# A local attention and squared-ReLU kernel: in the second block, the swap of the turned probabilities is issued at step 8 of each group in place of step 6 (last group: 5)

## The chip, the cores and the metric

The kernel runs on one core of a Trainium2 chip. Its engines work side by side, each through its own instructions in their order: TensorE (PE, with its weight loads PEld), VectorE (DVE), ScalarE (ACT), GpSimd (POOL) and SyncE (SP), which here does nothing but issue DMAs. The metric is the device time of one execution in microseconds (us). The three runs shown took 788.15, 789.97 and 790.61 us; the median is 789.97 us.

## The reference

Queries, keys and values come as 8 batches x 8 heads x 576 tokens x 64. Tokens are cut into chunks of 64, and each chunk attends to itself alone; the result goes through a two-layer MLP with a squared ReLU.

```python
scores = scale * np.matmul(q_c, k_c.transpose(0, 1, 2, 4, 3))
scores = scores - np.max(scores, axis=-1, keepdims=True)
attn = np.exp(scores)
attn = attn / (np.sum(attn, axis=-1, keepdims=True) + 1e-09)
out = np.matmul(attn, v_c)
...
x = np.ascontiguousarray(attn_out.transpose(0, 2, 1, 3)).reshape(B * S, H * D)
...
h = x @ w_in
r = np.maximum(h, 0.0)
g = s * (r * r) + b
return (g @ w_out).astype(np.float32)
```

There are 4608 tokens (36 blocks of 128), 512 features, and a hidden layer of 2048.

## The kernel before, in words

Everything is float32. A factor of a large product is split into a high and a low part, and three products (high by high, high by low, low by high) take the place of one.

The work is staged by tokens. A first stage handles 512 tokens and meanwhile prepares the weights. Then come four blocks of 1024 tokens. A block runs through steps: 12 matmuls of 128x512 each, first those of the up layer, then 28 of the down layer. Blocks two to four (class `Block`) use a scheme with seven products of half matrices in place of eight. The second stage, the first of the four blocks, is class `Second`, which is what the title calls the second block: its up layer takes 32 steps with the plain weights, and beside it DVE and ACT form the sums of weights that the later products need (`combine`, `combined_hi`, `combined_lo`) and send them to DRAM (`keep_combined`, line 200). All weights stand in DRAM as "kept" tiles; `stream` (line 428) requests them back, 512 KB at a time, into a pool of six buffers named `st`. A request has to wait until TensorE has done with the buffer's last tile.

While a block's steps run, the attention of the following block is computed in four groups of 256 tokens. For a group that starts at step n the table of `plan_attention` (line 580) puts: the loads of q, k and v at n - LEAD, the scores on TensorE at n, the row maximum and its subtraction (DVE) at n + 1, the exponential (ACT) at n + 2, the sum (DVE) at n + 3, the division and the turn (DVE, 32x32 transposes, `pB`, line 282) at n + 4, the swap at n + 6, and the products with the values (`values`, line 298, on TensorE) at n + VALUES, together with their copy out of PSUM by ACT. In `Second` the groups start at steps 4, 18, 30 and 41, and the values follow at n + 10.

The swap finishes the transpose that the turn began: eight DMAs of 64 KB within SBUF move 32-row pieces of `pB` into `pT` (line 291). They are issued by SP like every other large DMA: the requests of weights, the sending of the sums, the loads of q, k and v, the output.

What is written in one step is issued in the order of the list `pre[step]`, and `stream` comes behind it. An engine holds its instructions strictly in this order. SP's DMAs take eight semaphores in turn, and a DMA is issued only when the DMA eight places before it, which had the same semaphore, has landed.

Of the kernel before, what the change touches and what calls it, by code (L numbers as in the profile page):

```python
# [48 lines left out]
def local_attention_then_squared_relu_mlp(ctx: ExitStack, tc, qkv, w, s, b, out):  # L49
# [63 lines left out]
    class Pair:  # L113


        def __init__(self, k):
            self.layer, self.k = sequence[k]
            self.words = self.f = None
# [270 lines left out]

    class Block:  # L390
        UP, TILES, ORDER, GROUPS, LEAD, VALUES, END = 28, 56, (0, 2, 1, 3), (3, 14, 25, 36), 5, None, 9

        def __init__(self, n):
            self.tb0 = 4 + (n - 1) * BLOCK
# [41 lines left out]
        def place(self, layer, i):  # L436
            return PLACE[i]
# [142 lines left out]
        def plan_attention(self, n, a, after):  # L580

            self.at(max(n - self.LEAD, 0), a.load_qk, a.load_v)
            last = after is None
            end = ((self.END, a.values), (self.END + 1, a.x_out)) if last else ((self.VALUES or after - n, a.values, a.x_out),)
            for k, *fs in ((0, a.scores), (1, a.peak, a.sub), (2, a.exp), (3, a.sum), (4, a.norm, a.turn), (5 if last else 6, a.swap), *end):
                self.pre[n + k][:0] = fs

        def plan_following(self, following):
# [29 lines left out]
    class Second(Block):  # L618


        UP, TILES, ORDER, GROUPS, LEAD, VALUES, END = 32, 44, (0, 1, 2, 3), (4, 18, 30, 41), 7, 10, 10
        PLACES = 0, 1, 3, 2

        def operands(self, group, d):
# [8 lines left out]
        def place(self, layer, i):  # L633
            return super().place(layer, i) if layer else self.PLACES[i % 4]

# [275 lines left out]
```

## Time and profile before

| what | number |
|---|---|
| median of three runs | 789.97 us (788.15 to 790.61) |
| the profiled execution's own time | 787.95 us |
| its span, first to last instruction | 786.2 us |
| TensorE busy | 772.8 us, 98% of the span |
| DVE, ACT, POOL busy | 598.4, 444.8, 171.9 us |
| mean granted TensorE clock | 1.000 |

The profile is that of one execution, of 787.95 us. Busy time is what an engine spent in instructions; a wait is idle time ahead of an instruction, with the instruction or DMA that ended it. For a DMA the page gives the time from its issue to its landing. The second block runs from about 129 us to 305 us.

### The profile page before, as it was taken

How to read it: one execution, taken by the hardware profiler on the slowest of the kernel's cores; microseconds unless marked ns; L12 is line 12 of the kernel's file. 1: busy time of each engine (PE TensorE's matmuls, PEld its weight loads, DVE VectorE, ACT ScalarE, POOL GpSimd, SP SyncE). 2: the span in 40 equal slices, each digit the busy share in tenths (PEclk: the TensorE clock that was granted, in tenths of full speed). 3: DMA queues.
4: the chain of work that ended last, by engine and by line, in shares of the span. 5: the costliest groups of instructions: out<-in, count | busy, mean ns of one | idle time of the engine just before them, and what ended most of it. 6: DMA issues, size and time to landing. Idle time of an engine off the chain costs nothing.

```text
span 786.2 us, 13839 instructions
## 1 busy us (share of the span) xinstructions
PE 772.8 (98%) x5562; PEld 637.5 (81%) x5562; DVE 598.4 (76%) x610; ACT 444.8 (57%) x527; POOL 171.9 (22%) x74
## 2 busy tenths in 40 slices
PE   7899999999999999999999999999999999999998
PEld 7778788888887878888888888888888888888886
DVE  6898786978869894868799847786999646679752
ACT  4888774566663744555646444465654545565621
POOL 2444430000000240000374500002574101028000
PEclk9999999999999999999999999999999999999999
DMA  9999989889997588676665787857567665555653
GB/s 336 356 315 308 344 311 332 301 277 350 312 382 256 200 304 306 204 275 220 259 232 208 241 298 255 295 167 289 180 260 257 239 234 196 189 192 194 224 176 124
DMA packets 86978, 204.32 MB, mean 260 GB/s; under 512 B 7940, under 2 KB 38916, under 8 KB 86916
## 3 DMA queue, kind: packets, MB, share of 16 engines
q1 hardware_dynamic: 86768, 203.32, 74.1%
q8 instruction: 44, 0.72, 0.3%
q14 instruction: 18, 0.15, 0.1%
q10 hardware_dynamic: 148, 0.13, 0.0%
HBM read 156.24 MB, written 40.89 MB: 251 GB/s over the span
## 4 chain that ended last, share of the span: by engine, by line
PE 64%; DVE 1%; issue 1%; SPq 1%; DMA 0%; ACT 0%; DVEq 0%; ACTq 0%
PE ps_o L486 22%; PE ps_o L456 19%; PE ps L456 11%; PE ps L486 9%; PE ps_o L502 1%; PE ps_a L238 1%; PE ps_o L298 1%; SPq L291 1%; DMA st<-kept 0%; ACT gh L343 0%; PE ps L298 0%; DVE gl L344 0%; DVE pB L282 0%; DVE p L264 0%; DVE tmp L358 0%
## 5 line engine op out<-in xcount | busy, mean ns | idle before, releaser
L486 PE MATMUL ps_o<-gh,st 128*128 128x512 f32 x608 | 189.8, 390 | 0.3 <-DMA st<-kept 0.3
L344 DVE TENSOR_TENSOR gl<-q,gh 128x1024 fp32r<-128x1024 f32 x112 | 168.2, 1524 | 28.4 <-ACT gh L343 28.1
L473 POOL TENSOR_TENSOR q<-q 128x1024 f32<-128x1024 f32 x24 | 73.9, 3099 | 294.7 <-PE ps_a L238 179.1
L456 PE MATMUL ps_o<-xh,st 128*128 128x512 f32 x432 | 137.7, 389 | 0.0
L486 PEld LDWEIGHTS ps_o<-gh,st 128*128 128x128 f32 x608 | 114.1, 188 | 24.6 <-DMA st<-kept 0.4
L343 ACT CAST gh<-q 128x1024 fp32r<-128x1024 f32 x112 | 113.2, 1047 | 11.4 <-DVE q L473 10.7
L486 PE MATMUL ps_o<-gl,st 128*128 128x512 f32 x304 | 118.3, 389 | 0.0
L461 ACT ACTIVATE q<-q 128x1024 f32<-128x1024 f32 x48 | 50.9, 1061 | 80.3 <-DVE q L358 80.1
L456 PEld LDWEIGHTS ps_o<-xh,st 128*128 128x128 f32 x432 | 81.1, 188 | 16.9
L456 PE MATMUL ps_o<-xl,st 128*128 128x512 f32 x216 | 84.0, 389 | 0.0
L486 PE MATMUL ps<-gh,st 128*128 128x512 f32 x256 | 80.6, 390 | 0.8 <-DMA st<-kept 0.8
L456 PE MATMUL ps<-xh,st 128*128 128x512 f32 x240 | 79.5, 392 | 0.0
L679 ACT ACTIVATE o<-o,bias,sb 128x512 f32<-128x512 f32 x34 | 25.8, 808 | 91.4 <-DVE o L358 91.4
L413 POOL TENSOR_TENSOR xt<-xf 128x512 f32<-128x512 f32 x12 | 32.8, 2736 | 192.0 <-PE ps_o L486 137.7
L358 DVE TENSOR_TENSOR q<-ps_o,tmp 128x1024 f32<-128x1024 f32 x35 | 42.8, 1222 | 32.2 <-PE ps_o L456 27.9
L486 PEld LDWEIGHTS ps_o<-gl,st 128*128 128x128 f32 x304 | 57.1, 188 | 11.6
L152 POOL TENSOR_TENSOR f<-f,raw 128x1024 int32<-128x1024 int32 (+1 forms) x18 | 44.6, 2482 | 67.8 <-DVE f L146 24.0
L486 PEld LDWEIGHTS ps<-gh,st 128*128 128x128 f32 x256 | 48.0, 188 | 11.0 <-issue 0.9
L456 PEld LDWEIGHTS ps<-xh,st 128*128 128x128 f32 x240 | 45.0, 188 | 9.7
L358 DVE TENSOR_TENSOR tmp<-ps_o,tmp 128x1024 f32<-128x1024 f32 x30 | 36.6, 1219 | 20.9 <-PE ps_o L456 15.8
L473 DVE TENSOR_TENSOR q<-q 128x1024 f32<-128x1024 f32 x40 | 48.6, 1219 | 4.4 <-ACT q L462 3.7
L462 ACT ACTIVATE q<-q 128x1024 f32<-128x1024 f32 x48 | 51.0, 1062 | 1.5
(110 smaller groups left out, 1307.0 us busy)
## 6 DMA issues: line engine op xcount, KB each, us to landing
st<-kept SPq DMA_DIRECT2D x212, 512.0 KB, 5.1
qk<-in_qkv_dram SPq DMA_DIRECT2D x36, 512.0 KB, 6.1
raw<-in_w_dram SPq DMA_DIRECT2D x32, 512.0 KB, 6.9
kept<-wh SPq DMA_DIRECT2D x24, 512.0 KB, 8.3
kept<-wl SPq DMA_DIRECT2D x24, 512.0 KB, 8.7
v<-in_qkv_dram SPq DMA_DIRECT2D x36, 256.0 KB, 6.2
out_dram<-o SPq DMA_DIRECT2D x17, 512.0 KB, 3.1
pT<-pB SPq DMA_DIRECT2D x96, 64.0 KB, 2.2
```

Source lines behind the costliest of these rows:

```text
L152: nc.gpsimd.tensor_tensor(out=i, in0=i, in1=low.bitcast(I32), op=ALU.add)
L238: nc.tensor.matmul(out=self.ps[rows, h % 2, i * NHP + hp, :], lhsT=qk[cols, 0, hp, c, :], rhs=qk[cols, 1, hp, c, :], start=True, stop=True)
L343: nc.scalar.copy(out=hi[:, :, cols], in_=parts)
L344: nc.vector.tensor_tensor(out=lo[:, :, cols], in0=parts, in1=hi[:, :, cols].bitcast(F32), op=ALU.subtract)
L358: nc.vector.tensor_tensor(out=to, in0=self.ps[product], in1=x, op=ALU.add)
L413: engine.tensor_tensor(out=to, in0=x, in1=y, op=ALU.subtract)
L456: nc.tensor.matmul(out=to[:, k], lhsT=a[:, cols], rhs=x[:, c, :], start=c == 0 and n == 0, stop=c == 1 and n == 2)
L461: nc.scalar.activation(out=q, in_=q, func=AF.Relu)
L462: nc.scalar.activation(out=q, in_=q, func=AF.Square)
L473: engine.tensor_tensor(out=self.q[to, pp], in0=self.q[x, pp], in1=self.q[y, pp], op=ALU.subtract)
L486: nc.tensor.matmul(out=self.to[:, d], lhsT=a[:, cols], rhs=x[:, k, :], start=pp == 0 and k == 0 and n == 0, stop=pp == NPP - 1 and k == 1 ...
L679: nc.scalar.activation(out=to[:, d], in_=source[:, d], func=AF.Identity, scale=s_col, bias=bias[:, d0 + d:d0 + d + 1])
```

## The change

A table `SWAP` now gives the step of the swap, first for the groups that another group follows, then for the last one. For class `Block` it repeats the old numbers (6 and 5). For `Second` it is 8 and 8: three groups have their swap two steps later, the fourth three steps later.

```diff
     class Block:
         UP, TILES, ORDER, GROUPS, LEAD, VALUES, END = 28, 56, (0, 2, 1, 3), (3, 14, 25, 36), 5, None, 9
+        SWAP = 6, 5
...
-            for k, *fs in ((0, a.scores), (1, a.peak, a.sub), (2, a.exp), (3, a.sum), (4, a.norm, a.turn), (5 if last else 6, a.swap), *end):
+            for k, *fs in ((0, a.scores), (1, a.peak, a.sub), (2, a.exp), (3, a.sum), (4, a.norm, a.turn), (self.SWAP[last], a.swap), *end):
...
         UP, TILES, ORDER, GROUPS, LEAD, VALUES, END = 32, 44, (0, 1, 2, 3), (4, 18, 30, 41), 7, 10, 10
+        SWAP = 8, 8
```

No instruction is added or removed, and on PE, DVE, ACT and POOL the order stays. On SP the eight DMAs of the swap move in four places. The lines below the second insertion are numbered one or two higher in the changed kernel.

On SP, around the second group's swap (steps 23 to 27), before: `qk` and `v` are the loads of the third group, `st` the requests of the first two tiles of the down layer, `kept_1_81` and `kept_2_82` sums of weights on their way to DRAM.

```order
L215 DMA qk<-in_qkv_dram 128x1024 x2
L223 DMA v<-in_qkv_dram 128x512 x2
L291 DMA pT<-pB 32x512 x8
L432 DMA st<-kept_0_84 128x1024
L432 DMA st<-kept_1_85 128x1024
L200 DMA kept_1_81<-wh 128x4x256
L200 DMA kept_1_81<-wl 128x4x256
L200 DMA kept_2_82<-wh 128x4x256
```

The same place in the changed kernel, from the first request on, with the semaphores that each DMA waits for (DMAHW0 to DMAHW7 are the eight that DMAs take in turn):

```order
L433 DMA st<-kept_0_84 128x1024 [waits DMAHW4_49,PE_49]
L433 DMA st<-kept_1_85 128x1024 [waits DMAHW5_49,PE_49]
L200 DMA kept_1_81<-wh 128x4x256 [waits DMAHW6_49,Activation_49]
L200 DMA kept_1_81<-wl 128x4x256 [waits DMAHW7_49,DVE_49]
L291 DMA pT<-pB 32x512 [waits DMAHW0_49,DVE_49]
L291 DMA pT<-pB 32x512 [waits DMAHW1_49]
L291 DMA pT<-pB 32x512 [waits DMAHW2_49]
L291 DMA pT<-pB 32x512 [waits DMAHW3_49]
L291 DMA pT<-pB 32x512 [waits DMAHW4_49]
L291 DMA pT<-pB 32x512 [waits DMAHW5_49]
L291 DMA pT<-pB 32x512 [waits DMAHW6_49]
L291 DMA pT<-pB 32x512 [waits DMAHW7_49]
```

Two requests and one pair of sums, 512 KB each, now stand between the loads and the swap, and the last four swap DMAs share their semaphores with these four.

On SP, around the fourth group's swap (steps 44 to 50), before: all are requests of down-layer tiles but the swap.

```order
L432 DMA st<-kept_1_85 128x1024
L432 DMA st<-kept_2_86 128x1024
L291 DMA pT<-pB 32x512 x8
L432 DMA st<-kept_3_87 128x1024
L432 DMA st<-kept_0_84 128x1024
L432 DMA st<-kept_1_85 128x1024
L432 DMA st<-kept_2_86 128x1024
```

And now:

```order
L433 DMA st<-kept_1_85 128x1024
L433 DMA st<-kept_2_86 128x1024
L433 DMA st<-kept_3_87 128x1024
L433 DMA st<-kept_0_84 128x1024
L433 DMA st<-kept_1_85 128x1024
L291 DMA pT<-pB 32x512 x8
L433 DMA st<-kept_2_86 128x1024
```

Three requests moved in front of the swap. In the first group's place a pair of sums and the four loads of the second group (2.5 MB) moved in front of it; in the third group's two stores of the output and two requests (2 MB).

## Rows read from the trace of the kernel before

**Rows 1.** The page's head and its busy line: busy time, share of the span and count of instructions.

```profile
span 786.2 us, 13839 instructions
PE 772.8 (98%) x5562; PEld 637.5 (81%) x5562; DVE 598.4 (76%) x610; ACT 444.8 (57%) x527; POOL 171.9 (22%) x74
```

**Rows 2.** Who waited for whom, TensorE alone, 120 to 330 us: waiter, its line, what it waited for: total us, times, longest us.

```profile
PE ps L486 <- DMA st<-kept: 0.8, 1, 0.8
PE ps_o L486 <- DMA st<-kept: 0.3, 1, 0.3
```

**Rows 3.** TensorE in order of time: start, duration, line, out<-in, count, and in brackets the idle time before it. The values' products (L298) of the four groups, and the two matmuls that waited; last, from the chain of waits, 96 matmuls (8 steps) without a gap.

```profile
168.64 1.16 PE L298 MATMUL ps_a<-pT,v 64*64 64x64 f32 x64
...
209.36 1.16 PE L298 MATMUL ps_a<-pT,v 64*64 64x64 f32 x64
...
245.55 1.16 PE L298 MATMUL ps_a<-pT,v 64*64 64x64 f32 x64
...
251.04 0.50 PE L486 MATMUL ps_o<-gh,st 128*128 128x512 f32 x1 [0.29 <-DMA st<-kept]
...
278.51 1.16 PE L298 MATMUL ps_a<-pT,v 64*64 64x64 f32 x64
280.43 0.47 PE L486 MATMUL ps<-gh,st 128*128 128x512 f32 x1 [0.76 <-DMA st<-kept]
...
283.43 21.76 PE ps_o L486 x96
```

**Rows 4.** SP in order of time: start and duration of the issue, line, out<-in, count. The surroundings of the four swaps (L291).

```profile
151.06 1.69 SPq L432 DMA_DIRECT2D st<-kept  x2
155.55 5.51 SPq L291 DMA_DIRECT2D pT<-pB  x8
...
198.20 0.48 SPq L223 DMA_DIRECT2D v<-in_qkv_dram  x1
201.64 4.95 SPq L291 DMA_DIRECT2D pT<-pB  x8
206.69 1.03 SPq L432 DMA_DIRECT2D st<-kept  x2
...
231.29 1.74 SPq L432 DMA_DIRECT2D st<-kept  x2
236.57 6.81 SPq L291 DMA_DIRECT2D pT<-pB  x8
...
244.66 3.13 SPq L432 DMA_DIRECT2D st<-kept  x4
...
271.76 4.95 SPq L291 DMA_DIRECT2D pT<-pB  x8
276.81 2.96 SPq L432 DMA_DIRECT2D st<-kept  x6
```

**Rows 5.** DVE in order of time: the turns of the second and the fourth group.

```profile
200.37 1.25 DVE L282 STREAM_TRANSPOSE pB<-p 128x1024 f32<-128x1024 f32 x1
...
270.49 1.25 DVE L282 STREAM_TRANSPOSE pB<-p 128x1024 f32<-128x1024 f32 x1
```

**Rows 6.** DMA issues by line in narrow stretches: out<-in, count, KB each, us from issue to landing. In this order: the second request issued from 152.42 us; the v load issued at 198.20; the request issued at 231.29; the request issued at 244.66; a pair of sums issued from 161.16. Then the landing times (min/median/max) of the swaps issued from 201.64 and from 271.76.

```profile
st<-kept SPq DMA_DIRECT2D x1, 512.0 KB, 5.5
...
v<-in_qkv_dram SPq DMA_DIRECT2D x1, 256.0 KB, 7.8
...
st<-kept SPq DMA_DIRECT2D x1, 512.0 KB, 9.8
...
st<-kept SPq DMA_DIRECT2D x1, 512.0 KB, 6.3
...
kept<-wh SPq DMA_DIRECT2D x1, 512.0 KB, 3.2
kept<-wl SPq DMA_DIRECT2D x1, 512.0 KB, 4.8
...
DMA to landing us min/median/max: 2.0/3.8/4.7
...
DMA to landing us min/median/max: 2.0/2.0/2.0
```

**Rows 7.** Stretches: us, then busy time of PE, PEld, DVE, ACT, POOL with counts, the granted TensorE clock, the DMA engines' busy share, and GB/s.

```profile
156.00:162.00 6.00, 6.00 (x29) 4.95 (x28) 5.37 (x11) 3.04 (x3) 0.00 (x0) 1.00 0.44 120
162.00:168.00 6.00, 6.00 (x28) 4.99 (x27) 2.62 (x4) 3.97 (x4) 0.00 (x0) 1.00 0.97 287
192.00:198.00 6.00, 6.00 (x28) 4.95 (x28) 4.96 (x8) 3.80 (x5) 0.00 (x0) 1.00 0.88 249
198.00:204.00 6.00, 6.00 (x28) 4.99 (x27) 5.09 (x9) 0.99 (x2) 0.00 (x0) 1.00 1.05 395
```

**Rows 8.** TensorE's clock: the first matmuls of the run and some 10 us later the same shape (start, duration, count); a stretch behind the last matmul (columns as in rows 7); and TensorE's longest wait in the first 120 us (columns as in rows 2).

```profile
1.05 3.57 PE L107 MATMUL ps_h<-ones 128*128 128x128 f32 x16 [1.05 <-DVE one_col L93]
...
10.33 2.94 PE L107 MATMUL ps_h<-ones 128*128 128x128 f32 x24
...
785.00:787.00 2.00, 0.00 (x0) 0.00 (x0) 0.00 (x0) 0.00 (x0) 0.00 (x0) 0.73 0.00 0
...
PE ps_h L703 <- DVE g L716: 2.5, 2, 1.4
```

## The prediction

> **What bounds the kernel now.** I read the page's busy line first: TensorE is busy 772.8 of 786.2 us [rows 1]. What it does is not changed, so the time can only move by TensorE's idle time. The view of waits comes next, for TensorE alone and the second block: from 120 to 330 us it waited for a DMA twice, 0.8 and 0.3 us [rows 2]. In order of time these are 0.76 us ahead of 280.43 and 0.29 us ahead of 251.04, both for requested weights [rows 3]. More than 1.05 us cannot be won in this block. SP's timeline says where the two come from: SP stands at a swap until its turn is done (fourth group: the turn ends at 270.49 + 1.25 = 271.74, the swap starts at 271.76), spends 5 us on its eight issues, and only then hands out six requests, from 276.81 [rows 4, 5]. The request that landed at 251.0 (244.66 + 6.3) also stood behind a swap, the third [rows 4, 6]. The third thing to read is the other side: how long before the values' products a swap was complete. Those products start at 168.64, 209.36, 245.55 and 278.51 [rows 3]; a swap DMA lands 2.0 us or more after its issue [rows 6].
>
> **The change part by part.** No instruction is added, so durations stay; what moves is SP's order. For each group I follow two questions: do the requests that now go first remove a wait, and does the swap still land before its products?
>
> *Requests in front, third and fourth group.* The two waits of 0.29 and 0.76 us were for the first request behind a swap. Both requests now go ahead of it, several us before they are needed: gain 1.05 us, at the least 0. What is late next: the request now first behind the fourth swap goes out at 276.8 as the first one did, for a matmul three steps later; a step takes 21.76 / 8 = 2.72 us [rows 3], so it has 8.2 us more. Nothing.
>
> *Fourth group's swap.* It waited for the turn, not for its place. Three requests now precede it; the last needs TensorE to have finished step 47, which it does three steps before the values open step 51: 278.51 - 3 x 2.72, at about 270. The swap still starts at 271.76 with the turn and ends its landing at 276.12 + 2.0 = 278.1, before 278.51. Cost 0; the cover is thin (0.4 us), but it was thin before.
>
> *Second group's swap, the term that decides.* Before, SP was free at 198.7 and idled until the turn ended at 201.62 [rows 4, 5]. The eight issues took until 206.6 and the last landed at about 208.0, 1.3 us before the products at 209.36. Now two requests and a pair of sums go first. Their data are ready, and they leave between 198.7 and about 201.7. But the swap pays in another way: each of its DMAs waits until the DMA eight places before it has landed, as the semaphores in the order show, and for the last four these are now the four new ones, 2 MB. They queue behind the loads, whose last one landed at 198.20 + 7.8 = 206.0 [rows 6]. The stretch 198 to 204, where the DMA engines were full with loads and sums alike, moved 395 GB/s [rows 7], so 512 KB take 1.33 us, and four take 5.3: the last of the sums lands at 211.3. Then the eighth swap DMA goes, and lands 2.0 us later, at 213.3. TensorE, which holds its order, stands at the values from 209.36: 4.0 us. Nothing covers that: all later matmuls are queued behind them, and ACT's copy of the values and what DVE takes from later steps wait in turn. On SP the swap holds up more sums and the requests for tiles that TensorE needs from step 34 on, five steps later; and whoever takes over the buffer of `pB` stands some steps later in its engine's order too.
> The bounds: if the four had no queue before them and landed like a pair of sums in a nearly empty one (3.2 and 4.8 us [rows 6]), they would be down by about 206 and only SP's issues would count: the fourth swap DMA starts at 206.0 with the last load's landing, four more follow at 4.95 / 8 = 0.62 us, the last lands at 210.5, and the wait is 1.2 us. If they crawled as in 192 to 198 (249 GB/s, 2.1 us each [rows 7]), it would be 206.0 + 8.4 + 2.0 - 209.36 = 7.1 us. I take 4.0, by the row nearest in time and mix.
>
> The Trainium skill (DMA: Bandwidth & Descriptors, Anatomy of one DMA) gives a fixed cost of about 2.0 us for a DMA plus its bytes at 436 GB/s. The swaps that had the queue to themselves agree on the fixed part (2.0/2.0/2.0 in the fourth group [rows 6]). On the moving part the row says 395: by the page, as an estimate, four tiles take 4.8 us, the wait would be 3.5 us and the sum below +2.4.
>
> *First group's swap.* SP idled from 152.75 to 155.55 for the turn [rows 4]; now a pair of sums and four loads, 2.5 MB, leave in that gap, and the swap behind them. The last request before them landed at 152.42 + 5.5 = 157.9 [rows 6]. At 395 GB/s 2.5 MB take 6.6 us: 164.6, the last swap DMA lands at 166.6, two us before 168.64. At 287 GB/s (162 to 168 [rows 7]) it is 9.1 us, 169.0, and a wait of 0.4. I take 0, with 0.4 as the end. The DMA engines stood at 0.44 in 156 to 162 [rows 7], so the early requests use time that was lost.
>
> *Third group's swap.* The request at 231.29 landed 9.8 us later, at 241.1 [rows 4, 6], and one more request, two stores and two requests now stand between it and the swap's end: five times 1.33 gives 247.8, and 249.8 for the last swap DMA, against products at 245.55 + 4.0 = 249.55. But the wait of the second group lets the queue drain against TensorE, and with no backlog the limit is the second request: free when step 36 is done, three steps before the values (245.55 - 3 x 2.72 + 4.0 = 241.4), and down 5.5 to 6.3 us later [rows 6], 246.9 to 247.7, so that the swap ends at 248.9 to 249.7. So 0 to 0.3 beside the delay of the second group, and I take 0.
>
> The sum: + 4.0 - 1.05 = + 2.95 us, from the profiled execution's 787.95 to 790.9. That execution lies 2.0 us under the median of the runs (789.97); on the median the forecast is 792.9 us.
>
> **The rivals.**
> *A. The swap is in time and only the gain is left (not slower).* The mechanism: DMAs on one queue overlap enough that the four new ones land with the loads in front of them, not after. For it: sums in a nearly empty queue landed after 3.2 and 4.8 us [rows 6], and the DMA engines' share fell to 0.44 during a swap before, so there is room. Against it: the loads in front landed after 7.8 us, which is a queue. With the low bound's wait of 1.2 the sum is +0.15, 790.1 us; with none, 788.9. It decides at the landing of the second sum: at 207.3 or sooner the wait is gone.
> *B. More than one group is late.* If the queue runs at the slow rates in all places: 0.4 in the first group, 7.1 in the second, 0.3 in the third, less 1.05: +6.8, 796.7 us. For it: 249 and 287 GB/s stretches stand right beside two of the four places [rows 7]. Against: those stretches hold gaps in the supply, which the change fills.
> *C. The wait costs TensorE its clock.* In the run's first matmuls 16 of 128x128 took 3.57 us, 0.22 each; later 24 took 2.94, 0.12 each [rows 8]: the two levels, 1.2 and 2.4 GHz. TensorE's longest wait in the first 120 us was 1.4 us, and its clock stayed up; behind the last matmul the granted clock fell to a mean of 0.73 within 785 to 787 [rows 8]. A wait of 4.0 us lies between. If it brings the clock down for as long as the first burst lasted, 3.6 us, half of that is lost: 1.8 us on top, +4.75, 794.7 us. The Trainium skill (TensorE: Matmul & The Clock Gate, HAM oscillation — how this bites in real kernels) holds that a long enough wait for a DMA between matmuls takes the clock to half; by it this rival would be likely, and no row here shows such a wait.
>
> **How the numbers follow.** I give the forecast 0.55, A 0.22, B 0.11, C 0.12. A measurement of this kernel can tell 0.3%, 2.4 us, from no change. The forecast's own range is 791 to 795: waits of 2.1 to 6.1 us; about two thirds of it lie over +2.4. So slower gets 0.37 + 0.11 + 0.12 = 0.60; no change that can be told gets A but for a rest, and the lower third of the forecast, 0.36; faster 0.04, which would take a gain that no row offers. The range of 8 in 10 reaches down into A (789.2) and up to B's edge (796.4).
>
> **What would show it.** In the changed kernel's profile TensorE should wait once at L298 for `pT<-pB`, some 4 us at 209.4, and the two waits for `st<-kept` at 251 and 280 should be gone. SP's timeline should show the second swap's eight issues stretched from some 5 us to about 10, its last four spaced by the landings of requests and sums. The first and the fourth swap should land before their products. The prediction is wrong if L298 waits under 2 us in the second group, if it waits in the others too, or if the granted clock dips after the wait.

## The result, and the profile after

The changed kernel takes 799.48 us (median of four runs, 798.13 to 801.99), the kernel before beside it 789.59 us (788.15 to 790.61). The ratio is 1.0125, with a 95% interval of 1.0109 to 1.0141: slower by 9.9 us, where the forecast was 2.95 us and the upper end of its range 796.4. The profiled execution of the changed kernel took 800.75 us, against 787.95 for the one of before. Two executions that ran at a far lower clock throughout, one of a kernel below (1304.04 us, mean granted clock 0.557) and one of the kernel before beside the last runs (964.29 us, 0.754), are left out of the numbers here.

The page's head and its busy line, after (answers to [rows 1]):

```profile
span 798.9 us, 13836 instructions
PE 780.0 (98%) x5562; PEld 642.7 (80%) x5562; DVE 606.1 (76%) x610; ACT 445.0 (56%) x527; POOL 163.0 (20%) x74
```

The count of matmuls is the same, 5562, yet TensorE's busy time rose from 772.8 to 780.0 us. The span grew by 12.7 us, so over half of what was lost does not stand in idle time at all. That is the first thing to see here, and the one the prediction's first step excluded.

Who waited for whom, TensorE alone, 120 to 345 us, after (answers to [rows 2]; waiter, line, what it waited for: total us, times, longest us):

```profile
PE ps_a L298 <- DMA pT<-pB: 4.2, 3, 2.3
PE ps_a L298 <- DVE f L186: 1.6, 1, 1.6
```

Both waits for `st<-kept` are gone, and 5.8 us of waits at the values stand in their place. The second line names DVE's L186, but L298 reads only `pT` and `v`; what it stood for is the swap: the fourth of the eight swap DMAs, the last that the first four products need, landed at 212.05, and they start at 212.18.

TensorE in order of time, after (answers to [rows 3]; start, duration, line, out<-in, count, in brackets the idle time before). The values of the four groups; the second and third are cut in two by a second wait:

```profile
169.80 1.16 PE L298 MATMUL ps_a<-pT,v 64*64 64x64 f32 x64
...
212.18 0.33 PE L298 MATMUL ps_a<-pT,v 64*64 64x64 f32 x4 [1.59 <-DVE f L186]
213.70 1.97 PE L298 MATMUL ps_a<-pT,v 64*64 64x64 f32 x60 [1.19 <-DMA pT<-pB]
...
256.62 0.33 PE L298 MATMUL ps_a<-pT,v 64*64 64x64 f32 x4 [2.28 <-DMA pT<-pB]
257.71 1.97 PE L298 MATMUL ps_a<-pT,v 64*64 64x64 f32 x60 [0.76 <-DMA pT<-pB]
...
291.62 1.16 PE L298 MATMUL ps_a<-pT,v 64*64 64x64 f32 x64
```

The first and the fourth group did not wait. The second group's values stood 1.59 + 1.19 = 2.78 us, the third's 2.28 + 0.76 = 3.04 us. And 60 products took 1.97 us, where all 64 took 1.16 in the kernel before. The stretches around the ends of the two waits and behind them, after (us; busy time of PE, PEld, DVE, ACT, POOL with counts; granted TensorE clock; DMA engines' busy share; GB/s):

```profile
213.00:223.20 10.20, 9.50 (x82) 8.15 (x83) 6.04 (x9) 5.16 (x7) 0.00 (x0) 0.50 0.64 210
257.40:260.80 3.40, 3.09 (x63) 2.81 (x64) 0.00 (x0) 1.08 (x3) 0.00 (x0) 0.50 0.92 311
```

TensorE's clock stood at 0.50, the lower of its two levels, for 10.2 us at the first wait, of which the first 0.7 still lie in the wait, and for 3.4 us at the second, 0.3 of them in the wait. What that cost follows from when TensorE is ready for each group's values. Before, it is ready at 168.64, 209.36, 245.55 and 278.51 [rows 3]. After, at 169.80, 212.18 - 1.59 = 210.59, 256.62 - 2.28 = 254.34 and 291.62. The lag is 1.16, 1.23, 8.79 and 13.11 us.
- From the second to the third group it grows by 7.56: 2.78 of waiting and 4.8 of half clock (half of 9.50 busy us is 4.75).
- From the third to the fourth it grows by 4.32: 3.04 of waiting, less the 0.29 that is gone at before's 251.04, and 1.6 of half clock.
- The 1.16 us of the first group were there before any of the moved instructions could act; the first stage of these two executions differed by that.

The swap of the second group, in SP's order, after (answers to [rows 4]; start and duration of the issue, line, out<-in, count), with its seventh and eighth DMA once more by themselves, then the third group's:

```profile
199.81 0.89 SPq L433 DMA_DIRECT2D st<-kept  x2
200.81 0.37 SPq L200 DMA_DIRECT2D kept<-wh  x1
202.08 0.37 SPq L200 DMA_DIRECT2D kept<-wl  x1
206.83 5.35 SPq L291 DMA_DIRECT2D pT<-pB  x8
...
210.95 0.60 SPq L291 DMA_DIRECT2D pT<-pB  x1
211.59 0.59 SPq L291 DMA_DIRECT2D pT<-pB  x1
...
241.19 1.53 SPq L684 DMA_DIRECT2D out_dram<-o  x2
243.60 2.95 SPq L433 DMA_DIRECT2D st<-kept  x2
246.64 9.49 SPq L291 DMA_DIRECT2D pT<-pB  x8
```

DVE at the second group's turn, and the DMA issues of narrow stretches, after (KB each, us from issue to landing): the second sum issued at 202.08, and the third group's second request issued at 246.21:

```profile
201.52 1.25 DVE L282 STREAM_TRANSPOSE pB<-p 128x1024 f32<-128x1024 f32 x1
...
205.58 1.23 DVE L196 TENSOR_TENSOR wl<-f,wh 128x1024 fp32r<-128x1024 f32 x1 [1.12 <-ACT wh L192]
...
kept<-wl SPq DMA_DIRECT2D x1, 512.0 KB, 8.9
...
st<-kept SPq DMA_DIRECT2D x1, 512.0 KB, 9.4
```

In the third group the second request lands at 246.21 + 9.4 = 255.6; the last swap DMA leaves there (246.64 + 9.49 - 0.51 = 255.62, with 0.51 us for its own issue), and TensorE went on at 257.71. That is the hold by the semaphores which the prediction described for the second group.

In the second group itself that hold did not decide. The second sum lands at 202.08 + 8.9 = 211.0 (forecast: 211.3), and until then the eighth swap DMA could not have left. But SP was still issuing the seventh (210.95 to 211.55), and the eighth went out right behind it, at 211.59. The eight issues took 5.35 us, where they took 4.95 in the kernel before [rows 4]: they were hardly stretched. The swap ended late because it began late, not with the turn's end (202.77) but at 206.83, with the end of DVE's L196 (205.58 + 1.23). Asked for two steps later, `pT` had taken another buffer from the shared pool, and that DVE instruction was the last to use it; the run with a buffer of its own, below, bears this out. So there were two holds side by side, the buffer's to 211.6 and that of the DMAs in front to 211.0, and the first was not foreseen.

### The profile page after: what moved, and what is told of

Read it like the earlier page. It is cut to its first block, busy times and chain, and to the rows that moved or that the text cites. A ratio compares the mean times of both kernels' runs of the same rounds, so it can differ in the third digit from the quotient of the medians.

```text
span 798.9 us, 13836 instructions
## 1 busy us (share of the span) xinstructions
PE 780.0 (98%) x5562; PEld 642.7 (80%) x5562; DVE 606.1 (76%) x610; ACT 445.0 (56%) x527; POOL 163.0 (20%) x74
## 4 chain that ended last, share of the span: by engine, by line
PE 79%; DVE 8%; DMA 6%; ACT 4%; issue 2%; SPq 1%; POOL 0%; DVEq 0%; ACTq 0%; POOLq 0%
PE ps_o L487 26%; PE ps_o L457 18%; PE ps L457 10%; PE ps L487 10%; PE ps_h L705 4%; PE ps_o L730 3%; DMA raw<-in_w_dram 2%; DVE f L186 2%; DMA st<-kept 2%; DVE wl L196 2%; PE ps_a L238 1%; PE ps_o L503 1%; DMA kept<-wl 1%; PE ps L652 1%; PE ps_o L298 1%
## 5 line engine op out<-in xcount | busy, mean ns | idle before, releaser
L344 DVE TENSOR_TENSOR gl<-q,gh 128x1024 fp32r<-128x1024 f32 x112 | 172.3, 1560 | 39.6 <-ACT gh L343 39.2
L474 POOL TENSOR_TENSOR q<-q 128x1024 f32<-128x1024 f32 x24 | 74.0, 3102 | 303.8 <-DMA st<-kept 184.5
L414 POOL TENSOR_TENSOR xt<-xf 128x512 f32<-128x512 f32 x12 | 19.9, 1655 | 203.3 <-DVE gl L344 155.0
L487 PEld LDWEIGHTS ps<-gh,st 128*128 128x128 f32 x256 | 48.0, 188 | 10.2
L474 DVE TENSOR_TENSOR q<-q 128x1024 f32<-128x1024 f32 x40 | 48.5, 1218 | 4.4 <-ACT q L463 3.7
```

Source lines behind the costliest of these rows:

```text
L344: nc.vector.tensor_tensor(out=lo[:, :, cols], in0=parts, in1=hi[:, :, cols].bitcast(F32), op=ALU.subtract)
L474: engine.tensor_tensor(out=self.q[to, pp], in0=self.q[x, pp], in1=self.q[y, pp], op=ALU.subtract)
L487: nc.tensor.matmul(out=self.to[:, d], lhsT=a[:, cols], rhs=x[:, k, :], start=pp == 0 and k == 0 and n == 0, stop=pp == NPP - 1 and k == 1 ...
```

## The experiments

The theory that the runs were made for (T): each of the two swaps is late by the requests and sums in front of it, TensorE waits, and the wait brings its clock to half. All kernels below take the step of each group's swap from a table:

```diff
-        SWAP = 8, 8
+        SWAP = {4: 6, 18: 8, 30: 6, 41: 5}
```

The keys are the steps at which the groups start, the values the step of the swap; this one is the first run, in which the second group alone moves.

### One group at a time

> The kernel before, but with the second group's swap alone at step 8 (the others stay at 6, 6 and 5). Theory T (the late swap makes TensorE wait at the values, and the wait brings its clock to half for some time): TensorE waits at L298 in the second group for a pT DMA, about 2.8 us in all, the granted clock is 0.5 for about 10 us behind it, which costs about 4.8 us, and nothing else moves: 789.6 + 2.8 + 4.8 = about 797.2 us, 796 to 799. Rival R1 (the half clock has nothing to do with the wait): the same wait, no stretch at half clock, 791.5 to 793.5 us. Rival R3 (the third group is late only because the second was): the third group waits here too although its swap is at its old step, 799 us or more.

Measured: 798.01 us, ratio 1.0103 (1.0087 to 1.0118). TensorE in order of time, then the stretch behind, then the swap on SP and the landing of the second sum (issued at 201.28):

```profile
212.19 0.33 PE L298 MATMUL ps_a<-pT,v 64*64 64x64 f32 x4 [2.42 <-DMA pT<-pB]
214.71 1.97 PE L298 MATMUL ps_a<-pT,v 64*64 64x64 f32 x60 [2.20 <-DMA pT<-pB]
...
214.10:223.40 9.30, 8.69 (x80) 7.54 (x81) 3.71 (x7) 3.99 (x5) 0.00 (x0) 0.50 0.69 228
...
208.21 4.96 SPq L291 DMA_DIRECT2D pT<-pB  x8
...
kept<-wl SPq DMA_DIRECT2D x1, 512.0 KB, 9.5
```

A wait of 4.62 us and, in this view, 9.3 us at half clock, in the second group only. R1 falls (the clock goes with the wait), and so does R3 (the third group did not wait). The wait is longer than in the changed kernel, because TensorE was ready sooner (209.8) and the swap began later still (208.21, behind a reader on TensorE this time). Here the buffer's hold sets the lateness: the second sum has landed at 201.28 + 9.5 = 210.8, and the last swap DMA leaves at 208.21 + 4.96 - 0.59 = 212.58, at SP's own pace.

> The kernel before, but with the third group's swap alone at step 8. Theory T, in which each group's lateness comes from the requests in front of its own swap: TensorE waits 2 to 4 us at L298 in the third group, with half clock behind it for 3 us or more: 789.6 + 3 + 1.7 - 0.3 (the wait at before's 251.04 gone) = about 794, 792.5 to 798 us. Rival R3 (the third group was late in the changed kernel only because the second had been): its swap lands before the values, no wait at L298, no half clock, 789.0 to 789.6 us. The second group must not wait in either case.

Measured: 796.57 us, 1.0093 (1.0075 to 1.0112).

```profile
251.35 0.33 PE L298 MATMUL ps_a<-pT,v 64*64 64x64 f32 x4 [3.27 <-DMA pT<-pB]
252.55 1.50 PE L298 MATMUL ps_a<-pT,v 64*64 64x64 f32 x60 [0.86 <-DMA pT<-pB]
...
253.20:256.60 3.40, 3.40 (x37) 2.80 (x30) 1.18 (x2) 2.02 (x3) 0.00 (x0) 0.50 0.61 245
```

The third group is late by itself: 4.13 us of waiting and again 3.4 us at half clock, though the second group did not wait. So the zero which the prediction gave this group was wrong on its own ground.

### All four groups one step earlier

```diff
-        SWAP = 8, 8
+        SWAP = {4: 7, 18: 7, 30: 7, 41: 7}
```

> All four groups at step 7. In the second group the two requests go ahead of the swap and the pair of sums does not; in the third the two stores and one request. Theory T: the second group's last swap DMA waits for the second request's landing (208.3 in the changed kernel) and lands at about 210.5, a wait of about 1 us; the third group's waits for the one request (249.2 in the run with the third alone at 8) and lands at about 250, a wait of 2 to 4 us. The clock falls to half behind the longer wait only: 789.6 + 1 + 3 + 1.5 - 0.8 = about 794, 791.5 to 797 us. Rival R9 (any wait at the values brings the clock to half): half clock in the second group too, behind about 1 us, 797 to 800 us. Rival R10 (a step less is enough): no wait at L298, 788.5 to 789.6 us.

Measured: 794.35 us, 1.0051 (1.0033 to 1.0069). The two groups on TensorE, then the stretch at half clock behind the second group's values and a stretch around the third's:

```profile
211.87 0.33 PE L298 MATMUL ps_a<-pT,v 64*64 64x64 f32 x4 [0.95 <-DMA pT<-pB]
212.82 1.15 PE L298 MATMUL ps_a<-pT,v 64*64 64x64 f32 x60 [0.62 <-DMA pT<-pB]
...
251.27 0.33 PE L298 MATMUL ps_a<-pT,v 64*64 64x64 f32 x4 [0.60 <-DMA pT<-pB]
252.36 1.15 PE L298 MATMUL ps_a<-pT,v 64*64 64x64 f32 x60 [0.75 <-DMA pT<-pB]
...
214.80:218.20 3.40, 3.40 (x10) 2.72 (x10) 1.79 (x3) 3.20 (x4) 0.00 (x0) 0.50 1.03 337
250.00:256.00 6.00, 4.65 (x78) 3.60 (x78) 3.62 (x4) 2.02 (x3) 0.00 (x0) 1.00 0.73 240
```

1.57 us of waiting in the second group still brought the clock down, though the 60 products themselves ran at full speed and the fall came only behind them; 1.35 us in the third did not. The mean clock of the ten executions ran from 0.993 (795.79 us) to 1.000 (790.78 us), that of the kernel before never under 0.997: waits of this size, it seems, cost the clock in some executions and not in others. The time lies in T's range, but by luck: T had the half clock behind a wait of 2 to 4 us in the third group, and it came behind the second group's 1.57. R9 and R10 fall.

### Keeping TensorE busy while the swap comes

```diff
             tiles = [self.bank(2) for _ in range(N if apart else 1)]
+            for _ in range(self.fill):
+                nc.tensor.matmul(out=tiles[0][:, 0, 0:P], lhsT=ident, rhs=ident, start=True, stop=True)
```

> The changed kernel (all four groups at step 8) with 22 matmuls of the identity by itself (128x128, about 0.12 us each at full clock, 2.7 us in all) ahead of the values' products of the second and of the third group, into the tile that the values then overwrite. They need nothing that is late, so TensorE works while the swap comes. Theory T (the idle time brings the clock down): the granted clock stays at 1.0 in both places, the waits at L298 shrink to under 0.7 us each, and the time falls by the two losses at half clock, 4.8 and 1.7 us, to about 793, 791.5 to 795.5 us. Rival R1 (the half clock has another cause, or comes with any late swap): the half clock stays and the time is 798 us or more. Rival R4 (matmuls on so small a tile do not count as work for the clock): as R1, with the half clock beginning during the 22 matmuls or right behind them.

Measured: 797.41 us, 1.0099 (1.0082 to 1.0115), mean clock 1.000. A matmul of this kind stands as two records in the trace, so 22 took 5.08 us and not 2.7, which is why the time missed T's range. Even so the kernel's median is 2.1 us under the changed one's (the intervals of the two ratios just meet), although TensorE is kept from the values for 10.2 us in place of 5.8. The next two runs are one kernel, with 12 and 16 of them:

> As the run with 22 matmuls of the identity, but with 12 ahead of the second group's values and 16 ahead of the third's. In that run 22 of them took 5.08 us, 0.23 us each, so these are 2.8 and 3.7 us, about as long as TensorE stood idle there in the changed kernel (2.8 and 3.0 us). Theory T (idle time brings the clock down): granted clock 1.0 throughout, waits at L298 of 1.5 us at most, and the time lies 4.8 + 1.7 us under the changed kernel's less what the longer filling adds, 793 to 796 us. Rival R1 (the half clock comes with the late swap, filled or not): a stretch at 0.5 and 798 us or more.

> One more look at the kernel with 12 and 16 filling matmuls, for a profile. Theory T: granted clock 1.0 from 120 to 300 us, the waits at L298 under 1.5 us, 794 to 797 us. Rival R1: a stretch at 0.5 behind the second group's values.

Measured: 795.06 us as the median of five runs (ratio 1.0077, 1.0054 to 1.0100), and 795.73 us in the profiled execution. TensorE at the two places, and the stretches there:

```profile
210.37 2.84 PE L299 MATMUL ps_a<-ident 128*128 128x128 f32 x24
213.15 0.33 PE L302 MATMUL ps_a<-pT,v 64*64 64x64 f32 x4
213.89 1.15 PE L302 MATMUL ps_a<-pT,v 64*64 64x64 f32 x60 [0.41 <-DMA pT<-pB]
...
249.95 3.74 PE L299 MATMUL ps_a<-ident 128*128 128x128 f32 x32
...
209.00:224.00 15.00, 14.59 (x197) 12.54 (x196) 10.13 (x16) 9.48 (x11) 0.00 (x0) 1.00 0.82 251
250.00:262.00 12.00, 11.94 (x185) 10.29 (x184) 7.58 (x7) 3.87 (x6) 0.00 (x0) 1.00 0.35 111
```

The swap is as late as before, the values start as late (213.15 and 213.89, against 212.18 and 213.70), but TensorE works meanwhile and its clock stays at 1.00. This is the run that separates the delay from the clock: 799.48 - 795.06 = 4.4 us come back with nothing changed but work that nobody needs, and R1 and R4 fall. The intervals of the two ratios do not meet, and the mean clocks of the runs fit: 0.996 to 1.000 in these five, 0.989 to 0.993 in the four of the changed kernel. What is left, 795.06 - 789.68 = 5.4 us, is about what the waits come to (2.78 + 3.04 - 1.05 = 4.8); that it is the delay is not shown more closely.

### The buffer, or the requests in front

> The changed kernel, but pT takes its buffer at step 6 (fourth group 5) as in the kernel before, and only the DMAs go out at step 8. In the changed kernel the second group's first swap DMA went out at 206.83, with the end of the DVE instruction that had last read the buffer (205.58 + 1.23), 4 us after the turn; the last went out at 211.59, just behind the landing at 211.01 of the DMA eight places before. Theory T (the four new DMAs in front of the swap hold its last four issues): the first swap DMA goes out with the turn, at about 203, but the last still behind 211.0, its landing moves by 0.5 us at most, the wait and the half clock stay, 798.0 to 800.0 us. Rival R8 (the buffer makes the swap late): the whole swap moves up by 4 us, the second group does not wait, no half clock there, 791 to 794 us.

Measured: 800.36 us, 1.0127 (1.0103 to 1.0151). The edit (a `hold` that takes `pT` at step 6) missed its aim: the swap still began at 207.25, with the end of the same DVE instruction, presumably because the first group's later swap had already shifted which buffer was free. So this run tells nothing of R8. The next gives `pT` a buffer of its own:

```diff
-    slots = ctx.enter_context(tc.tile_pool(name="slots", bufs=45))
+    slots = ctx.enter_context(tc.tile_pool(name="slots", bufs=44))
+    turned = ctx.enter_context(tc.tile_pool(name="turned", bufs=1))
...
-            pT = slot(name="pT")
+            pT = turned.tile([P, 2, DM], F32, name="pT") if self.own else slot(name="pT")
```

> The changed kernel (all four at step 8), but the second block's pT has a buffer of its own (one is taken from the 45 shared ones), so that no swap waits for another tile's reader. The kernel that took pT's buffer early did not do that: its second swap still began with the end of the same DVE instruction, 207.25 against a turn that was done at 203.2. Theory T (the four new DMAs hold the swap through the semaphores): the first swap DMA goes out with the turn, at about 203, the last four stay behind the landings of the two requests and the two sums (207 to 211), the last one lands at about 213; the wait is shorter by 0.6 us, the half clock stays, 797.5 to 800 us. Rival R8 (the buffer made the swap late): no wait in the second group, 791 to 795 us.

Measured: 801.09 us, 1.0141 (1.0115 to 1.0166). SP around the swap, the second sum's landing (issued at 202.80), and TensorE:

```profile
204.09 8.41 SPq L294 DMA_DIRECT2D pT<-pB  x8
...
kept<-wl SPq DMA_DIRECT2D x1, 512.0 KB, 9.2
...
213.30 0.33 PE L301 MATMUL ps_a<-pT,v 64*64 64x64 f32 x4 [2.38 <-DMA pT<-pB]
214.20 1.97 PE L301 MATMUL ps_a<-pT,v 64*64 64x64 f32 x60 [0.57 <-DMA pT<-pB]
```

Now the swap begins at 204.09, one us behind the turn, and it takes 8.41 us to issue where the changed kernel took 5.35: its last DMA leaves at 204.09 + 8.41 - 0.51 = 211.99, as soon as the second sum has landed (202.80 + 9.2 = 212.0). The wait is 2.95 us. So without the buffer's hold the DMAs in front hold the swap by the semaphores, as the prediction had it, and R8, by which the second group would be in time, falls. But the buffer is not without effect: in the changed kernel's profile and in the run with the second group alone it was the hold that lasted longer, and each of the two is enough to make TensorE wait. That with the buffer's hold and nothing in front the group would be late too was not run; it follows from those two profiles, where the last swap DMA left after the second sum had landed. The time lies above T's range. The six executions run from 798.48 us at a mean clock of 0.996 to 804.33 at 0.989, and the clock is not all of that: another at 0.990 took 800.07.

### The part that seemed to pay

> The first and the fourth group's swap at step 8, the second and third at their old step 6. Theory T: no wait at L298 anywhere; of the two waits for requested weights the one of 0.76 us goes (it stood behind the fourth swap) and the one of 0.29 us stays (it stood behind the third): 789.6 - 0.8 = 788.8 us, 788.0 to 789.6. Rival R5 (the first group's swap, complete only 0.16 us before its products in the changed kernel, is late by itself): a wait of 0.1 to 0.5 us there, and 789.0 to 790.5 us. Rival R6 (the requests won by the fourth group were not on the path): the 0.76 us turns up at another matmul, 789.6 us.

> Only the fourth group's swap at step 8, its pT buffer taken at step 5 as before; the others at 6. Theory T: the one part of the change that paid. The wait of 0.76 us for the request behind the fourth swap goes and nothing else moves: 789.6 - 0.8 = 788.8 us, 788.0 to 789.4. Rival R6 (the freed time is given back): as with the first and fourth group at 8, where DVE took a wl or gl later beside GpSimd, TensorE waits for DVE by about 1 us instead: 789.4 to 790.4 us.

Measured: 790.09 us, 1.0009 (0.9998 to 1.0019), and 790.04 us, 1.0011 (0.9996 to 1.0026). No swap is late, the 0.76 us behind the fourth swap are gone, and nothing is won: in both, TensorE waits for another thing. From the first, TensorE, DVE and GpSimd:

```profile
276.13 0.50 PE L487 MATMUL ps<-gl,st 128*128 128x512 f32 x1 [1.01 <-DVE gl L344]
...
260.64 2.30 DVE L474 TENSOR_TENSOR q<-q 128x1024 f32<-128x1024 f32 x1
...
259.59 2.27 POOL L414 TENSOR_TENSOR xt<-xf,xt 128x512 f32<-128x512 f32 x1
```

L474 takes 2.30 us, for 1.22 in the kernel before. GpSimd's third and fourth `xt` no longer wait for DVE, the likely reason being that the later swap changed which buffer a tile takes. The fourth ends at 259.59 + 2.27 = 261.86, and L474 1.1 us behind it, as if the two took turns. In the kernel before GpSimd came second (its third `xt` from 258.65, for 2.20 us, DVE's subtraction from 258.48, for 1.22) and DVE lost nothing. DVE is now 1.1 us late through the group, and `gl` with it. R6 is right. The wait behind the third swap, 0.29 us in the kernel before, is 0.48 and 0.78 us in these two profiles.

> Swaps at 6, 6, 6 and, in the fourth group alone, 8, with pT in a buffer of its own. In the two runs with the fourth group at 8 and the second and third at 6, the wait of 0.76 us went, but TensorE waited 1.0 us for a DVE instruction (gl, L344): GpSimd's third xt had got another buffer, no longer waited for DVE and ran beside DVE's subtraction (L474), which took 2.30 us in place of 1.22. Here the order shows GpSimd's third xt waiting for DVE again. Theory T2 (that collision gave the gain back): the wait for gl is gone too, 789.6 - 0.8 = 788.8 us, 788.0 to 789.4. Rival R11 (something else makes gl late, or the other buffers bring a new wait): 789.4 to 791 us.

Measured: 789.55 us, 1.0000 (0.9989 to 1.0011). The wait for `gl` is gone as T2 says, and the same subtraction (L477 there) takes 1.21 us. But now the wait that was 0.29 us at before's 251.04 is 1.2:

```profile
253.85 0.50 PE L490 MATMUL ps_o<-gh,st 128*128 128x512 f32 x1 [1.20 <-DMA st<-kept]
```

The request it waits for stands behind the third swap, as before. That swap took 7.38 us to issue here, for 6.81 in the kernel before; why the DMAs landed later this run does not tell. R11 holds in its second half.

### The swap on another engine's queue

```diff
-                        nc.sync.dma_start(out=pT[64 * c + 32 * k:...
+                        self.queue.dma_start(out=pT[64 * c + 32 * k:...
```

> The kernel before (steps 6, 6, 6, 5), but the second block's swaps are issued by GpSimd, which has little else to do there, in place of SP. SP then never stands at a swap, and the swap's DMAs are not tied to the landing of SP's. Theory T: both waits for requested weights (0.29 and 0.76 us) go and the swaps land in time, 789.6 - 1.05 = 788.5 us, 787.7 to 789.2. Rival R12 (GpSimd's issues take longer or hold up DVE beside it): a wait at L298 in one group or more, and 790 to 800 us.

> The kernel before (steps 6, 6, 6, 5) with the third and the fourth swap of the second block issued by GpSimd; the first and second stay on SP. With all four on GpSimd both waits for requested weights were gone and only the second group was late (2.6 us: its swap began at 204.13, 0.6 us behind the turn's end, and landed late). Theory T: both waits go, no wait at L298, 789.6 - 1.05 = 788.5 us, 787.8 to 789.2. Rival R13 (another wait takes their place, as in the two runs with the fourth group at 8): 789.4 to 791 us, with a wait for DVE, ACT or a request of 0.4 to 1.2 us between 245 and 300 us.

> The same with the third and fourth swap issued by ACT in place of GpSimd. Theory T: the waits for requested weights go, 788.5 us, 787.8 to 789.2. Rival R14 (ACT, which waits for the turn and then issues eight DMAs in some 5 us, is late with the copies and halves that TensorE needs): waits for ACT of 1 us or more in the third or fourth group, 790 to 796 us.

Measured: 795.49 us (1.0067, 1.0044 to 1.0089), 795.48 us (1.0068, 1.0053 to 1.0082) and 798.68 us (1.0108, 1.0092 to 1.0123). With all four on GpSimd the waits for `st` are gone, and the second group waits 2.6 us, at a mean clock of 0.996. With the third and fourth alone there, the third waits 0.51 + 2.11 = 2.6 us. TensorE, and the DMA issues of 236 to 248 us, of the second run:

```profile
249.89 1.18 PE L300 MATMUL ps_a<-pT,v 64*64 64x64 f32 x60 [2.11 <-DMA pT<-pB]
...
st<-kept SPq DMA_DIRECT2D x4, 512.0 KB, 11.1
pT<-pB POOLq DMA_DIRECT2D x8, 64.0 KB, 7.0
```

GpSimd issued the third swap 0.65 us behind the turn, in 4.23 us, and its DMAs followed each other without a wait. Its 64 KB pieces still took 7.0 us to land (5.4 for the same swap in the kernel before), because SP, no longer held up by the swap, had sent its stores and requests into the same DMA engines: the stores from 235.72 and the requests from 238.24, where the kernel before sent its requests from 244.66 [rows 4]. So the swap's place in SP's order did two things in the kernel before: it held back the requests, which cost 0.3 and 0.8 us, and it kept their megabytes out of the swap's way, which is worth more. R12 is right in outcome but not in its reason: GpSimd's issues took less time than SP's. T and R13 both fail in the second run: the new wait is the swap's own, 2.6 us, and the time is 4 us above R13's range. With ACT issuing, the eight issues of the third swap took 7.75 us, its last piece landed at 252.4, and the values stood 5.25 us; R14's wait for ACT came too, 1.3 us, but it is the smaller part, and the time lies above its range. The Trainium skill (DMA: Bandwidth & Descriptors, Issuing engines are not separate DMA queues) says that DMAs of all issuing engines run on the same 16 DMA engines and mix there; the 7.0 us agree.

### The stretch at half clock

> The changed kernel, with the four bias products (eight records of 128x1 in the trace, L859) at step 26 in place of 28, so that they run ahead of the second group's values and 128x512 matmuls follow the values directly, as in the third group. Theory C1 (the narrow matmuls behind the wait prolong the half clock): the stretch at 0.5 behind the second group's values shrinks from 10.2 us to 3 to 7 us, and the time falls by half of that, 796 to 798.5 us. Rival C2 (the length of the wait or the place sets the stretch): it stays at 9 to 11 us and the time at 799 to 800.5 us. The waits at L298 stay in both.

Measured: 801.39 us, 1.0141 (1.0121 to 1.0160). TensorE, and the stretch at half clock:

```profile
209.09 1.84 PE L859 MATMUL ps_o<-one_col,t 128*128 128x1 f32 x8 [3.87 <-DVE t L853]
...
207.80:214.50 6.70, 5.41 (x17) 4.66 (x18) 5.96 (x12) 4.06 (x4) 0.00 (x0) 0.50 0.84 273
```

The edit does not tell C1 from C2: two steps earlier the biases wait 3.87 us for DVE's column sums, and by then the second group's swap is in time. But here TensorE stood for something other than a DMA, and the clock fell just the same, for 6.7 us, the first 1.3 of them still in the wait. The run with a buffer of its own has a shorter case in its first stage, with no swap near it. TensorE waits for DVE, and the clock at half behind it:

```profile
31.35 0.50 PE L708 MATMUL ps_h<-xh,wh 128*128 128x512 f32 x1 [1.84 <-DVE g L721]
...
32.80:36.20 3.40, 3.40 (x9) 2.66 (x9) 2.50 (x3) 1.82 (x3) 2.76 (x2) 0.50 1.07 386
```

At the same place the kernel before waited 1.38 us and kept its clock.

Why the second group pays 10.2 us at half clock and the third 3.4 stays open. It is not the place alone: the second group had 3.4 us with all swaps at step 7 and 6.7 with GpSimd issuing, the third 6.7 in this very run, where 128x512 matmuls follow its values directly. Nor is it the length of the wait alone: 4.13 us idle in the third group brought 3.4 us at half clock, 2.78 in the second 10.2.

## Why the prediction was wrong

- **What bounds the kernel.** TensorE, rightly. But "the time can only move by TensorE's idle time" is the step that failed first: its busy time rose by 7.2 us with the same matmuls, for a part of them ran at half clock.
- **The two waits, gain 1.05.** Both are gone in the changed kernel. That they are a gain by themselves is not shown: three kernels that took one away without a late swap came out at 1.0000 to 1.0011, each with a new wait of 1.0 to 1.2 us.
- **Fourth group 0, first group 0.** Right: no wait at 291.62 and 169.80.
- **Second group 4.0.** The number was near, by luck in part. The second sum landed at 211.0 for 211.3 and the last swap DMA at 213.6 for 213.3, but what held that DMA in the changed kernel was the late start of the swap, for which `pT`'s new buffer is the reason; the prediction named no such hold. Its own sign, eight issues stretched to about 10 us, is missing (5.35). The mechanism that it described is real, as the run with a buffer of its own shows (8.41 us, the last DMA right at the second sum's landing). The wait was 2.78 us, inside the bounds of 1.2 to 7.1, and smaller than 4.0 mainly because TensorE came 1.23 us later in that execution. The figures that the prediction quotes from the Trainium skill (DMA: Bandwidth & Descriptors, Anatomy of one DMA) are given there for DMAs that GpSimd issues; the sum does not use them.
- **Third group 0.** This term failed: 3.04 us. The second request went out three steps before the values, as forecast (254.34 - 3 x 2.72 = 246.2), but it landed after 9.4 us, not after 5.5 to 6.3. The assumption that the queue would have drained by then was wrong, and with the second group in time the wait was 4.13 us. Rival B had this group late, but by 0.3 us.
- **Rival C.** It named what weighed most and got 0.12. Its size was 1.8 us, for one wait; measured are 4.8 and 1.6 us, for two. The Trainium skill's section named beside it (TensorE: Matmul & The Clock Gate, HAM oscillation — how this bites in real kernels), by which the rival was likely, agrees with every profile here whose wait at the values was 2.6 us or longer; the clock also fell behind waits of 1.57 us there and 1.84 us in the first stage. The prediction weighed it down because a wait of 1.4 us in the first stage had left the clock up [rows 8], which says nothing of one of 3 to 4: no step of the sum had a term for the clock.

The sum in its own terms: 2.78 + 3.04 - 1.05 = 4.8 us of waits, for 2.95 forecast, and 6.4 us of half clock, for 0: 11.2. The two profiled executions lie 12.8 us apart, 1.2 of it from the first stage, and the medians 9.9; the four executions of the changed kernel spread over 3.9 us. No kernel tried beats the one before by more than a run can tell.

## What to carry to other kernels

Price a wait of TensorE twice: the idle time, and then the matmuls behind it at half clock, which here cost 4.8 us behind a wait of 2.78 and 1.6 behind one of 3.04; if the wait can't be removed, matmuls on data that are ready can keep the clock, as they did here. Before requests are moved ahead of a small urgent transfer, take the landing time of the last of them, with what is queued before it, from the trace: a small transfer standing in front is also what keeps the queue short for itself. And a tile that is asked for at another step may take another buffer, so that waits turn up on engines that the change doesn't name: look for the buffer's last reader before the cause that you expected is called the cause.

## What was not expected of the hardware

The lower clock cost more than the waits (6.4 against 5.8 us), and around a wait of 2.78 us that was broken by four matmuls it lasted 10.2 us, around an unbroken 3.87 us 6.7. A DVE operation that began while GpSimd was in one of the same kind took 2.30 us in place of 1.22, and TensorE waited 1.0 us some 15 us later. And 64 KB swap DMAs issued from an otherwise idle queue took 7.0 us to land behind another queue's requests, against 2.0 us in a free one [rows 6].
